# Spreading row gathers over expert blocks, and moving key and value copies to ScalarE, in an attention and mixture-of-experts kernel

## The chip, the cores and the metric

The kernel runs on one core of a Trainium2 chip. A core has five engines with instruction streams of their own: TensorE (PE in the profile; its weight loads are PEld), VectorE (DVE), ScalarE (ACT), GpSimd (POOL) and SyncE (SP), the last of which only issues DMA transfers here. They wait for each other through semaphores. The metric is the time of one execution on the device in microseconds (us); lower is better. All data is float32.

## The reference

Two stages follow each other. The first is attention with a local window and a few global keys, the second a mixture of eight experts in which each token goes to exactly one expert and none is dropped.

```python
# attention: q, k, v are (4, 8, 768, 64); n_global = 8, n_local = 96
scores = q @ k.T / sqrt(64)
rel = pos[:, None] - pos[None, :]
is_global = pos[None, :] < n_global
is_local = (rel >= 0) & (rel < n_local)
keep = is_global | is_local
dist = where(is_global & ~is_local, n_local, abs(rel))
scores = where(keep, scores - slope[h] * dist, -1e9)
out = softmax(scores) @ v
x = out.transpose(0, 2, 1, 3).reshape(3072, 512)

# experts: w_gate (512, 8), w1 (8, 512, 1024), w2 (8, 1024, 512)
logits = x @ w_gate
expert_idx = argmax(logits, axis=1)
gate_w = softmax(logits)[arange(N), expert_idx]
for e in range(8):                       # rows of each expert
    h = maximum(x[expert_idx == e] @ w1[e], 0)
    y[expert_idx == e] = h @ w2[e]
out = gate_w[:, None] * y
```

## The kernel before

Attention goes through 16 pairs of heads (4 batches, 4 pairs each) in three steps per pair, 48 steps in all. A step covers two blocks of 128 queries. Its work is a pipeline over steps: the score products of step n, the attend products (probabilities times values) of step n-2, the transposes of step n-4. As the window is shorter than a block, each block of queries needs its own key block and the one before, whose first 16 columns are replaced by the 16 first keys (the global ones). These replaced copies are `kA` for the keys and `va` for the values; GpSimd makes them:

```python
def keys_at(kT, kA, a0, a1):
    nc.gpsimd.tensor_copy(out=kA[:, a0:a1, GW:P], in_=kT[...][:, :, GW:P])
    nc.gpsimd.tensor_copy(out=kA[:, a0:a1, 0:GW], in_=kT[:, 0:GW]...to_broadcast(...))

def turn_v(pr):
    nc.gpsimd.tensor_copy(out=to, in_=vh[:, :, 0:VA])
    nc.gpsimd.tensor_copy(out=to[0:GW, ...], in_=vh[0:GW, ...].to_broadcast(...))

def scores(n):
    ...                                   # score products into PSUM
    nc.scalar.activation(e, ps, AF.Exp, scale=D ** -0.5)
    if c == 0:
        nc.vector.tensor_tensor(out=e, in0=e, in1=W[...], op=ALU.mult)
    else:
        for h in range(2):                # one mask product per head
            nc.vector.tensor_tensor(out=eh, in0=eh, in1=W[:, 2 * j + h, P:3 * P]..., op=ALU.mult)
```

Attention writes its rows to `x_tok` in device memory. When the last batch is routed, the kernel knows which rows belong to which expert. It fetches them by gathers: an indirect DMA that GpSimd issues, 128 pieces of 512 bytes each, through a list of row numbers. Expert 0 has its first 256 rows computed early (in pieces called by `work(...)`, two blocks at a time), as filler in the tail of attention. The tail and the gathers:

```python
def gather(xq, cols, n, top=N):
    for i in range(n):
        nc.gpsimd.indirect_dma_start(out=xq[:, i, :], in_=x_tok[...], in_offset=...cols[:, i:i + 1]...)

def take(p):                              # all the gathers of expert p, at once
    if p < E:
        xqs[p] = xq_s[p % 2]
        gather(xqs[p], rows_s[...], pieces_of(CAPS[r + 1]))     # 9 to 13 gathers

# ---- tail of attention (nu = 48 steps) ----
turn_x(xe_0, xq_0[0], TB)                 # VectorE turns gathered rows
turn(nu - 3)
attend(nu - 1)
turn_x(xe_0[:, :, P:2 * P], xq_0[1], TB)
work(2)
turn(nu - 2); logits(nu - 3); turn(nu - 1)
work(1)
logits(nu - 2); logits(nu - 1)
work(1)
...                                       # routing, with work pieces between
fetch_0(1)                                # 7 gathers: expert 0's other rows
settle(); work(1); rows_of(...)
take(1)                                   # 13 gathers: expert 1
...
work(3)
turn_x(xe_0, xq_0[0], TB)
work(4)
turn_x(xe_0[:, :, P:2 * P], xq_0[1], pieces_of(C0) - TB)
while later: later.pop(0)()               # two scatters of finished rows
```

Each expert has a hidden product with eight blocks, each followed by a ReLU on ScalarE, and a result product with four blocks, each copied out by VectorE. PSUM holds three blocks of each. The rows of a result are turned back by TensorE, scaled by VectorE and scattered to the output by GpSimd (`turn`), after the first block of the next hidden product. The weights of the next expert come in by SyncE (`fetch`).

```python
def hidden(p, between=None):
    for fc in range(FC):                  # FC = 8
        for kc in range(KC):
            nc.tensor.matmul(ph[:, 0:C], lhsT=w1t[...], rhs=xe[:, kc, 0:C], ...)
        nc.scalar.activation(hT[:, fc, 0:C], ph[:, 0:C], AF.Relu)
        if fc == 0 and between:
            between()                     # turn(): scale and scatter the rows before

def result(p):
    for dc in range(KC):                  # KC = 4
        for fc in range(FC):
            nc.tensor.matmul(po[:, 0:C], lhsT=w2t[...], rhs=hT[:, fc, 0:C], ...)
        nc.vector.tensor_copy(out=yT[:, dc, 0:C], in_=po[:, 0:C])
    return turn

fetch(1, 0); fetch(1, 1); ground()
sort(1)                                   # VectorE turns expert 1's rows
take(2)
hidden(0)
turn = result(0)
for p in range(1, E):
    hidden(p, turn)
    fetch(p + 1, 0)
    sort(p + 1)
    take(p + 2)
    turn = result(p)
    fetch(p + 1, 1)
```

Of the kernel before, what the change touches and what calls it, by code (L numbers as in the profile page):

```python
# [11 lines left out]
AF = mybir.ActivationFunctionType  # L12
# [11 lines left out]
NQ = 4  # L24
# [5 lines left out]
def kernel(  # L30
# [169 lines left out]
    def pieces_of(c):  # L200
        return (c + 31) // 32
# [50 lines left out]
    def rows_of(ps, nm, ns, mw, to_rows):  # L252
# [3 lines left out]
        nc.vector.tensor_scalar(out=to_rows, in0=pw, scalar1=float(NJ), scalar2=j_of[:, 0:1], op0=ALU.mult, op1=ALU.add)  # L256

    def gather(xq, cols, n, top=N):

        for i in range(n):  # L260
            nc.gpsimd.indirect_dma_start(out=xq[:, i, :], out_offset=None, in_=x_tok[0:NJ * top, :],  # L261
                                         in_offset=bass.IndirectOffsetOnAxis(ap=cols[:, i:i + 1], axis=0),
                                         bounds_check=NJ * top - 1, oob_is_err=False)

# [4 lines left out]

    def take(p):  # L270
        if p < E:
            r = ORDER[p] - 1
            xqs[p] = xq_s[p % 2]
            gather(xqs[p], rows_s[:, NQ * TB * r:NQ * TB * r + NQ * TB], pieces_of(CAPS[r + 1]))

# [51 lines left out]
    def banded_attention():  # L327
        with ExitStack() as actx:
# [71 lines left out]
            def turn_v(pr):  # L400
                vt = vts[pr % NV]
                va = vas[pr % 2]
                to = va[:, 0:2 * VA].rearrange("p (h x) -> p h x", h=2)
                vh = vt[:, 0:2 * VT].rearrange("p (h x) -> p h x", h=2)
                nc.gpsimd.tensor_copy(out=to, in_=vh[:, :, 0:VA])  # L405
                nc.gpsimd.tensor_copy(
                    out=to[0:GW, :, VW:VA].rearrange("p h (c w) -> p h c w", w=VW),
                    in_=vh[0:GW, :, 0:VW].rearrange("p h (o w) -> p h o w", o=1).to_broadcast([GW, 2, NB - 2, VW]))
# [43 lines left out]
            def scores(n):  # L452
                b, j, c = units[n]
                qT, kT, kA, _, _ = pairs[b * NJ + j]
# [12 lines left out]
                if n == 0:  # L467
                    turn_first(2, NB, ps_s.tile([P, 2, 512], F32, tag="s", name="first_1"))
                elif c == 1 and b == 0 and j + 1 < NJ:
                    weights(j + 1)  # L470
                if c == 0:
                    nc.vector.tensor_tensor(out=e[:, :, 0:w], in0=e[:, :, 0:w], in1=W[:, 2 * j:2 * j + 2, 0:w],
                                            op=ALU.mult)
                else:
                    for h in range(2):
                        eh = e[:, h, :].rearrange("p (t c) -> p t c", t=2)
                        nc.vector.tensor_tensor(  # L477
                            out=eh, in0=eh,
                            in1=W[:, 2 * j + h, P:3 * P].rearrange("p (o c) -> p o c", o=1).to_broadcast([P, 2, 2 * P]),
                            op=ALU.mult)  # L480
                st[n] = e

            def attend(n):
                b, j, c = units[n]
                _, _, _, vt, va = pairs[b * NJ + j]
                pt = st.pop(n)
# [229 lines left out]
            weights(0)  # L716
            turn_v(0)
            nu = len(units)
# [5 lines left out]
            for n in range(nu + 1):  # L724
# [234 lines left out]
    with tc.manual_schedule():  # L959
# [18 lines left out]
        with ExitStack() as ectx:  # L978
# [29 lines left out]
            def hidden(p, between=None):  # L1008
# [4 lines left out]
                for fc in range(FC):  # L1013
                    ph = ps_h.tile([P, 512], F32, tag="ph", name=f"ph_{p}_{fc}")
                    for kc in range(KC):
                        nc.tensor.matmul(ph[:, 0:C], lhsT=w1t[:, 0, kc, P * fc:P * fc + P], rhs=xe[:, kc, 0:C],  # L1016
                                         start=(kc == 0), stop=(kc == KC - 1))
                    nc.scalar.activation(hT[:, fc, 0:C], ph[:, 0:C], AF.Relu)  # L1018
# [8 lines left out]
            def result(p):  # L1027
# [31 lines left out]
            sort(1)  # L1059
            take(2)  # L1060
            hidden(0)
            turn = result(0)
            pf = ps_t.tile([P, DM], F32, tag="pt", name="pf")
            nc.tensor.matmul(pf[:, 0:1], lhsT=ones, rhs=bad, start=True, stop=True)
            nc.vector.tensor_scalar(out=bad_i, in0=pf[:, 0:1], scalar1=P - 0.5, scalar2=None, op0=ALU.is_lt)
            for p in range(1, E):
                hidden(p, turn)
                fetch(p + 1, 0)
                sort(p + 1)
                take(p + 2)  # L1070
                turn = result(p)
# [71 lines left out]
```

## Time and profile before

| | before |
|---|---|
| time, median of 3 runs | 591.25 us (590.97 to 591.64) |
| span of the profiled execution | 589.4 us |
| mean granted TensorE clock | 0.964 |
| score and attend products begin in earnest | 14.0 us |
| early pieces of expert 0 begin | 182.3 us |
| hidden product of expert 0 (remaining rows), first matmul | 222.4 us |
| its result product, first matmul | 260.2 us |
| result product of expert 7, end of its matmuls | 578.5 us |

The page of a profile has a table of busy times, then the span in 40 equal slices whose digits are tenths of busy time (9 is 90% or more), then groups of instructions by source line. A line such as `L1018 ACT ACTIVATE hT<-ph` names source line, engine, operation, output and input tile. In the view in order of time the first column is the start and the second the duration, both in us; brackets give how long the engine had been idle and what ended that. In the table of windows there are, for each stretch, its length, the busy time of PE, PEld, DVE, ACT and POOL with counts, the granted clock, the share of the DMA engines and GB/s. In the table of waits the numbers are total us, times and longest us; "remote" stands for a releaser that the profile cannot name. Matmul ends are modelled, not recorded.

```profile
q1 hardware_dynamic: 137344, 58.16, 47.4%
q0 software_dynamic: 5264, 12.59, 6.7%
```

These are the DMA queues: packets, MB and share of the 16 engines. The second is GpSimd's, which carries the gathers and scatters.

### The profile page before, as it was taken

Reading aid. Unit: us, or ns where it says so; the run is one execution under the profiler, and the core shown is the slowest. Engines: PE = TensorE matmul, PEld = TensorE weight load, DVE = VectorE, ACT = ScalarE, POOL = GpSimd, SP = SyncE. Lnnn points to the kernel's source line nnn. Section 1 sums busy time; section 2 is a strip of 40 time slices with the busy share of each in tenths; the row PEclk is TensorE's granted clock in tenths of the full one; section 3 lists DMA queues with packets and bytes.
Section 4 is the critical chain, followed back from the end, with each engine's and each line's share of the span. In section 5 each row is a group of like instructions: output and inputs, shape, how many; then the busy total and the mean of one; then the engine's idle time right before and its main releaser. Section 6 shows DMA issues by size and latency. Waiting matters only on the chain.

```text
span 589.4 us, 8006 instructions
## 1 busy us (share of the span) xinstructions
PE 532.9 (90%) x3066; PEld 386.7 (66%) x3066; DVE 205.5 (35%) x537; ACT 101.4 (17%) x197; POOL 176.8 (30%) x227
## 2 busy tenths in 40 slices
PE   3999999999999985089999999999999969999993
PEld 2998988988988834087555555555555747666662
DVE  3886886876862533003003101301301302102011
ACT  2544334333332100010100100110110100100100
POOL 4332214231243077702701720710640640101001
PEclk9999999999999997579999999999999979999998
DMA  9999999999503087129173353562534737201001
GB/s 146 146 143 185 233 186 152 231 144 181 158 12 133 2 172 239 49 54 259 53 149 125 112 114 88 188 123 44 207 82 90 220 75 186 92 1 39 13 1 55
DMA packets 145184, 71.95 MB, mean 122 GB/s; under 512 B 126656, under 2 KB 126660, under 8 KB 145136
## 3 DMA queue, kind: packets, MB, share of 16 engines
q1 hardware_dynamic: 137344, 58.16, 47.4%
q0 software_dynamic: 5264, 12.59, 6.7%
q10 hardware_dynamic: 2528, 0.59, 0.7%
q8 instruction: 26, 0.43, 0.3%
q14 instruction: 22, 0.18, 0.1%
HBM read 59.00 MB, written 12.65 MB: 122 GB/s over the span
## 4 chain that ended last, share of the span: by engine, by line
PE 75%; another core or an unknown queue 11%; DVE 5%; DMA 3%; SPq 2%; issue 1%; ACT 1%; POOL 1%; ACTq 0%; POOLq 0%; DVEq 0%
PE po L1043 26%; PE ph L1016 24%; PE o L495 10%; PE s L463 7%; PE ph L298 3%; PE px L511 2%; PE pt L1052 2%; SPq L362 2%; DMA vt<-in_v_dram 1%; DVE y L287 1%; PE pi L603 1%; PE pq L526 1%; DMA x_tok<-xr 1%; PE pl L539 1%
## 5 line engine op out<-in xcount | busy, mean ns | idle before, releaser
L1045 DVE COPY yT<-po 128x416 f32<-128x416 f32 (+4 forms) x32 | 16.9, 529 | 280.9 <-PE po L1043 280.9
L1016 PE MATMUL ph<-xe,w_first 128*128 128x208 f32 (+3 forms) x256 | 80.8, 477 | 25.5 <-ACT hT L1018 18.7
L261 POOL DMA_INDIRECT xq_s<-x_tok,rows_s x85 | 85.1, 1001 | 25.9 <-issue 24.4
L1043 PE MATMUL po<-hT,w_second 128*128 128x416 f32 (+3 forms) x256 | 81.2, 478 | 5.6 <-ACT hT L1018 5.6
L1016 PEld LDWEIGHTS ph<-xe,w_first 128*128 128x128 f32 x256 | 51.1, 204 | 53.5 <-ACT hT L1018 19.3
L1018 ACT ACTIVATE hT<-ph 128x416 f32<-128x416 f32 (+4 forms) x64 | 29.8, 467 | 324.9 <-PE ph L1016 212.9
L279 POOL DMA_INDIRECT out_dram<-y,idx_s x25 | 24.2, 969 | 204.3 <-DVE y L287 200.9
L1016 PE MATMUL ph<-xe,w_second 128*128 128x416 f32 (+3 forms) x256 | 79.7, 470 | 0.0
L1043 PE MATMUL po<-hT,w_first 128*128 128x208 f32 (+3 forms) x256 | 75.5, 456 | 0.0
L1043 PEld LDWEIGHTS po<-hT,w_second 128*128 128x128 f32 x256 | 49.5, 194 | 36.7 <-issue 10.2
L495 PE MATMUL o<-vt,e 128*128 128x128 f32 x384 | 72.1, 276 | 0.0
L1016 PEld LDWEIGHTS ph<-xe,w_second 128*128 128x128 f32 x256 | 48.3, 190 | 28.6 <-issue 9.8
L1043 PEld LDWEIGHTS po<-hT,w_first 128*128 128x128 f32 x256 | 47.8, 190 | 27.1 <-issue 10.0
L495 PE MATMUL o<-va,e 128*128 128x128 f32 x320 | 62.7, 278 | 0.0
L466 ACT ACTIVATE e<-s 128x1024 f32<-128x1024 f32 (+1 forms) x48 | 45.6, 951 | 94.3 <-issue 47.3
L495 PEld LDWEIGHTS o<-vt,e 128*128 128x128 f32 x384 | 57.0, 192 | 1.5 <-issue 1.0
L477 DVE TENSOR_TENSOR e<-e,Wb 128x512 f32<-128x512 f32 x64 | 45.3, 750 | 15.4 <-ACT e L466 15.2
L495 PEld LDWEIGHTS o<-va,e 128*128 128x128 f32 x320 | 48.5, 192 | 2.6 <-issue 2.5
L463 PE MATMUL s<-qT,kT 64*128 64x128 f32 x384 | 40.7, 290 | 0.9 <-ACT qT L397 0.9
L463 PE MATMUL s<-qT,kA 64*128 64x128 f32 x320 | 35.6, 300 | 3.6 <-POOL kA L381 3.6
L463 PEld LDWEIGHTS s<-qT,kT 64*128 64x128 f32 x384 | 30.8, 196 | 2.8 <-ACT qT L397 1.3
L405 POOL COPY va<-vt 128x650 f32<-128x650 f32 x16 | 14.6, 913 | 57.1 <-DMA vt<-in_v_dram 46.8
(163 smaller groups left out, 433.7 us busy)
## 6 DMA issues: line engine op xcount, KB each, us to landing
w_second<-in_moe_w_dram SPq DMA_DIRECT2D x16, 512.0 KB, 9.5
w_second<-in_moe_w_dram SPq DMA_DIRECT2D x4, 2048.0 KB
x_tok<-xr SPq DMA_DIRECT2D x24, 256.0 KB, 3.5
w_first<-in_moe_w_dram SPq DMA_DIRECT2D x12, 512.0 KB, 7.7
w_first<-in_moe_w_dram SPq DMA_DIRECT2D x3, 2048.0 KB
vt<-in_v_dram SPq DMA_DIRECT2D x31, 192.0 KB, 4.7
qb<-in_q_dram SPq DMA_DIRECT2D x60, 96.0 KB, 4.3
kb<-in_k_dram SPq DMA_DIRECT2D x60, 96.0 KB, 3.7
```

Of the source, the lines that this page charges most:

```text
L261: nc.gpsimd.indirect_dma_start(out=xq[:, i, :], out_offset=None, in_=x_tok[0:NJ * top, :], in_offset=bass.IndirectOffsetOnAxis(ap=cols[:, ...
L279: p = nc.gpsimd.indirect_dma_start(out=out[:, :], out_offset=bass.IndirectOffsetOnAxis(ap=where, axis=0), in_=y[0:rows, :], in_offset=None ...
L298: nc.tensor.matmul(ph[:, P * f:P * f + P], lhsT=w1_0[:, 0, kc, c0:c0 + P], rhs=xe_0[:, kc, P * q:P * q + P], start=(kc == 0), stop=(kc == ...
L405: nc.gpsimd.tensor_copy(out=to, in_=vh[:, :, 0:VA])
L463: nc.tensor.matmul(ps[:, h, P * m:P * m + P], lhsT=lhsT, rhs=qT[r, P * i:P * i + P], start=True, stop=True)
L466: nc.scalar.activation(e[:, :, 0:w], ps[:, :, 0:w], AF.Exp, scale=D ** -0.5)
L477: nc.vector.tensor_tensor(out=eh, in0=eh, in1=W[:, 2 * j + h, P:3 * P].rearrange("p (o c) -> p o c", o=1).to_broadcast([P, 2, 2 * P]), op= ...
L495: nc.tensor.matmul(po[:, t, h, :], lhsT=pt[:, h, P * m:P * m + P], rhs=(vt if own else va)[:, c0:c0 + P], start=(m == mine[0][0]), stop=(m ...
L1016: nc.tensor.matmul(ph[:, 0:C], lhsT=w1t[:, 0, kc, P * fc:P * fc + P], rhs=xe[:, kc, 0:C], start=(kc == 0), stop=(kc == KC - 1))
L1018: nc.scalar.activation(hT[:, fc, 0:C], ph[:, 0:C], AF.Relu)
L1043: nc.tensor.matmul(po[:, 0:C], lhsT=w2t[:, 0, fc, P * dc:P * dc + P], rhs=hT[:, fc, 0:C], start=(fc == 0), stop=(fc == FC - 1))
L1045: nc.vector.tensor_copy(out=yT[:, dc, 0:C], in_=po[:, 0:C])
```

## The change

Three things are changed together.

1. `take(p)` is split. `plan(p)` only puts the gathers of an expert on a list, and `pace(n, after)` issues n of them, each made to wait for a given instruction: one after each ReLU of a hidden product (all that are left after the last), two after the first copy of a result product and one after each other. Expert 1's gathers are still issued at once by `take(1)`. The plan for expert 2 comes after `hidden(0)`. It is meant to keep GpSimd's queue from holding long dense runs of gathers.
2. The key and value copies go from GpSimd to ScalarE, one step later each, and the mask of a step is multiplied by one instruction for both heads. It is meant to keep GpSimd away from VectorE's operands in attention.
3. In the tail the three early pieces of expert 0 that stood around the last turns are put behind them, and the transposes of gathered rows are put together.

```diff
+    pending = []
+
+    def plan(p):
         if p < E:
             r = ORDER[p] - 1
             xqs[p] = xq_s[p % 2]
-            gather(xqs[p], rows_s[:, NQ * TB * r:NQ * TB * r + NQ * TB], pieces_of(CAPS[r + 1]))
+            cols = rows_s[:, NQ * TB * r:NQ * TB * r + NQ * TB]
+            for i in range(pieces_of(CAPS[r + 1])):
+                pending.append((xqs[p], cols, i))
+
+    def pace(n, after):
+        for _ in range(min(n, len(pending))):
+            g = gather_one(*pending.pop(0))
+            tc.add_manual_dep(g.ins, after.ins.name, ...Sync, DATA...)
+
+    def take(p):
+        plan(p)
+        while pending:
+            gather_one(*pending.pop(0))
...
             def keys_at(kT, kA, a0, a1):
-                nc.gpsimd.tensor_copy(out=kA[:, a0:a1, GW:P],
+                nc.scalar.copy(out=kA[:, a0:a1, GW:P],
...
-                nc.gpsimd.tensor_copy(out=kA[:, a0:a1, 0:GW],
+                nc.scalar.copy(out=kA[:, a0:a1, 0:GW],
...                                       # the two value copies likewise
-                keys_at(kT, kA, 0, NB - 1)          # in turn_qk, at c == 0
...
                 if n == 0:
                     turn_first(2, NB, ...)
+                    turn_v(0)
...
-                    for h in range(2):
-                        eh = e[:, h, :].rearrange("p (t c) -> p t c", t=2)
-                        nc.vector.tensor_tensor(out=eh, in0=eh, in1=W[:, 2 * j + h, P:3 * P]..., op=ALU.mult)
+                    eh = e.rearrange("p h (t c) -> p h t c", t=2)
+                    nc.vector.tensor_tensor(out=eh, in0=eh, in1=W[:, 2 * j:2 * j + 2, P:3 * P]..., op=ALU.mult)
...
                 if n < nu and c == 1 and pr + 1 < B * NJ:
+                    keys_at(*pairs[pr + 1][1:3], 0, NB - 1)
+                if n < nu and c == 2 and pr + 1 < B * NJ:
                     turn_v(pr + 1)
...
-            turn_x(xe_0, xq_0[0], TB)
             turn(nu - 3)
             attend(nu - 1)
-            turn_x(xe_0[:, :, P:2 * P], xq_0[1], TB)
-            work(2)
             turn(nu - 2)
             logits(nu - 3)
+            turn_x(xe_0, xq_0[0], TB)
+            turn_x(xe_0[:, :, P:2 * P], xq_0[1], TB)
             turn(nu - 1)
-            work(1)
+            work(3)
             logits(nu - 2)
             logits(nu - 1)
...
             turn_x(xe_0, xq_0[0], TB)
+            turn_x(xe_0[:, :, P:2 * P], xq_0[1], pieces_of(C0) - TB)
             work(4)
-            turn_x(xe_0[:, :, P:2 * P], xq_0[1], pieces_of(C0) - TB)
...
-                    nc.scalar.activation(hT[:, fc, 0:C], ph[:, 0:C], AF.Relu)
+                    done = nc.scalar.activation(hT[:, fc, 0:C], ph[:, 0:C], AF.Relu)
                     if fc == 0 and between:
                         between()
+                    pace(1 if fc < FC - 1 else len(pending), done)
...
-                    nc.vector.tensor_copy(out=yT[:, dc, 0:C], in_=po[:, 0:C])
+                    pace(2 if dc == 0 else 1, nc.vector.tensor_copy(out=yT[:, dc, 0:C], in_=po[:, 0:C]))
...
-            take(2)
             hidden(0)
+            plan(2)
             turn = result(0)
...
                 sort(p + 1)
-                take(p + 2)
+                plan(p + 2)
                 turn = result(p)
```

More of the change, by code (lines that the diff above doesn't have):

```diff
@@ L256, in rows_of, with gather_one @@
         nc.vector.tensor_scalar(out=to_rows, in0=pw, scalar1=float(NJ), scalar2=j_of[:, 0:1], op0=ALU.mult, op1=ALU.add)
+    def gather_one(xq, cols, i, top=N):
+        return nc.gpsimd.indirect_dma_start(out=xq[:, i, :], out_offset=None, in_=x_tok[0:NJ * top, :],
+                                            in_offset=bass.IndirectOffsetOnAxis(ap=cols[:, i:i + 1], axis=0),
+                                            bounds_check=NJ * top - 1, oob_is_err=False)
     def gather(xq, cols, n, top=N):
         for i in range(n):
-            nc.gpsimd.indirect_dma_start(out=xq[:, i, :], out_offset=None, in_=x_tok[0:NJ * top, :],
-                                         in_offset=bass.IndirectOffsetOnAxis(ap=cols[:, i:i + 1], axis=0),
-                                         bounds_check=NJ * top - 1, oob_is_err=False)
+            gather_one(xq, cols, i, top)
     def turn_x(xe, xq, n):
@@ L268, in turn_x @@
             nc.vector.transpose(xe[:, :, 32 * i:32 * i + 32], xq[:, i, :].rearrange("p (k q) -> p k q", k=KC))
-    def take(p):
+    pending = []
+    def plan(p):
         if p < E:
@@ L273, in take @@
             xqs[p] = xq_s[p % 2]
-            gather(xqs[p], rows_s[:, NQ * TB * r:NQ * TB * r + NQ * TB], pieces_of(CAPS[r + 1]))
+            cols = rows_s[:, NQ * TB * r:NQ * TB * r + NQ * TB]
[4 more added lines that the diff above has]
+            g = gather_one(*pending.pop(0))
+            tc.add_manual_dep(g.ins, after.ins.name, mybir.DependencyInfo(mybir.DependencyClass.Sync, mybir.DependencyReason.DATA),
+                              reason="spreads the gathers over the experts' work")
+    def take(p):
+        plan(p)
+        while pending:
+            gather_one(*pending.pop(0))
     scatters = []
@@ L404, in turn_v @@
                 vh = vt[:, 0:2 * VT].rearrange("p (h x) -> p h x", h=2)
-                nc.gpsimd.tensor_copy(out=to, in_=vh[:, :, 0:VA])
-                nc.gpsimd.tensor_copy(
+                nc.scalar.copy(out=to, in_=vh[:, :, 0:VA])
+                nc.scalar.copy(
                     out=to[0:GW, :, VW:VA].rearrange("p h (c w) -> p h c w", w=VW),
@@ L453, in scores @@
                 b, j, c = units[n]
-                qT, kT, kA, _, _ = pairs[b * NJ + j]
+                qT, kT, kA = pairs[b * NJ + j][0:3]
                 bl = blocks(c)
@@ L474, in scores @@
                 else:
-                    for h in range(2):
-                        eh = e[:, h, :].rearrange("p (t c) -> p t c", t=2)
[L477 to L480, printed above, removed]
+                    eh = e.rearrange("p h (t c) -> p h t c", t=2)
+                    nc.vector.tensor_tensor(
+                        out=eh, in0=eh,
+                        in1=W[:, 2 * j:2 * j + 2, P:3 * P].rearrange("p h (o c) -> p h o c", o=1).to_broadcast([P, 2, 2, 2 * P]),
+                        op=ALU.mult)
                 st[n] = e
@@ L484, in attend @@
                 b, j, c = units[n]
-                _, _, _, vt, va = pairs[b * NJ + j]
+                vt, va = pairs[b * NJ + j][3:5]
                 pt = st.pop(n)
@@ L716, in banded_attention @@
             weights(0)
-            turn_v(0)
             nu = len(units)
```

## The prediction

> **What bounds the kernel now.** I read the page's busy table and its 40 slices first. TensorE is busy nearly everywhere, with one hole:
>
> ```profile
> PE 532.9 (90%) x3066; PEld 386.7 (66%) x3066; DVE 205.5 (35%) x537; ACT 101.4 (17%) x197; POOL 176.8 (30%) x227
> ...
> PE   3999999999999985089999999999999969999993
> ...
> POOL 4332214231243077702701720710640640101001
> ```
>
> A slice is 14.7 us. Slices 1 to 12 are attention, 13 to 15 the routing tail with early pieces of expert 0, the rest the eight experts (numbered here by their place in the order, 0 to 7). The hole is slices 15 and 16 (the 8, 5 and 0), and POOL is dense there; a second dip (the 6) is in slice 32, again beside POOL. Second, the table of waits names who held the hole:
>
> ```profile
> ACT hT L1018 <- remote: 70.6, 9, 26.7
> ```
>
> This line is ScalarE's ReLU of the first expert product, waiting for something that the profile cannot name. Third, ScalarE alone in order of time, first around the hole, then around the dip:
>
> ```profile
> 204.14 0.38 ACT L300 ACTIVATE hT<-ph 128x256 f32<-128x256 f32 x1 [2.91 <-PE ph L298]
> 231.23 0.34 ACT L1018 ACTIVATE hT<-ph 128x208 f32<-128x208 f32 x1 [26.71 <-remote]
> 252.14 0.34 ACT L1018 ACTIVATE hT<-ph 128x208 f32<-128x208 f32 x1 [20.56 <-remote]
> ```
>
> ```profile
> 465.66 0.40 ACT L1018 ACTIVATE hT<-ph 128x272 f32<-128x272 f32 x1 [1.44 <-issue]
> 469.13 0.40 ACT L1018 ACTIVATE hT<-ph 128x272 f32<-128x272 f32 x1 [3.07 <-remote]
> 472.71 0.40 ACT L1018 ACTIVATE hT<-ph 128x272 f32<-128x272 f32 x1 [3.18 <-remote]
> 477.69 0.40 ACT L1018 ACTIVATE hT<-ph 128x272 f32<-128x272 f32 x1 [4.58 <-remote]
> 481.94 0.40 ACT L1018 ACTIVATE hT<-ph 128x272 f32<-128x272 f32 x1 [3.86 <-remote]
> ```
>
> The second ReLU waits for TensorE alone in the program. In the order of time TensorE began block 0 at 222.36, and blocks 0 to 2 stand as done by 228.5; yet their ReLUs run at 231.23, 252.14 and 254.29. With three PSUM buffers TensorE can do block 3 and then stops until 252.53. Fourth, the dense stretch in the table of windows:
>
> ```profile
> 235.00:250.00 15.00, 0.00 (x0) 0.00 (x0) 0.00 (x0) 0.00 (x0) 11.65 (x12) 0.50 0.19 52
> ```
>
> Every compute engine is idle and only POOL works, at gathers. The POOL rows of that stretch are 13 gathers from 233.45 to 250.11; the stuck ReLU goes 2.0 us after the last one ends. Around the dip 12 gathers run from 464.17 to 479.53, and the last stuck ReLU goes at 481.94, 2.4 us later. Experts 2 to 4 show the same on a small scale: expert 4's last gather ends at 434.9, its last ReLU comes at 437.25, some 3 us late, without cost, as TensorE has other work. Expert 1's 13 gathers (278.73 to 295.4) delayed nothing. So: **signals from TensorE reach ScalarE late while a dense run of gathers is on, and are through about 2.4 us after the run.** Why the hardware does so no row tells; I take it as a regularity of this trace. The signals to VectorE are late too beside the first 8 gathers (171.7 to 182.6): the normalisations at 180.78 and 183.81 follow products whose rows ended about 2 us and 3 us earlier.
>
> **What the Trainium skill says.** "Perfetto Trace Analysis", section "DMA Instruction — SWDGE (GPSIMD)": the end of a GpSimd DMA in a profile is that of descriptor generation, not of the transfer. The trace agrees: a gather's row is 1.00 us, and its consumers go later. The same page, "Tensor Engine Instruction (MATMUL, LD_WEIGHTS)": a matmul's end is computed, and its semaphore is pushed only once PSUM has acknowledged. So a finished row at 228.5 doesn't prove that the signal had left; this fits the trace, which proves neither. "SBUF — State Buffer", "Who interferes with whom": a VectorE instruction with two SBUF inputs contends with a GpSimd instruction that reads SBUF. It agrees: the pair of mask products at 33.44 took 2.30 us beside POOL's value and key copies, and takes 1.29 us undisturbed. No page I found bears on late TensorE signals.
>
> **The change, part by part.**
>
> *Gathers of expert 2, out of the first hidden product.* Before, all 13 stand on POOL right after the first scatters and so beside hidden(0). After, they follow hidden(0), paced by result(0) and hidden(1). But 7+13 gathers for experts 0 and 1 stay in one run: before, 204.76 to 230.5, then two scatters to 233.1. So the first ReLU still comes at about 231. What follows is freed once the remaining run is through: at best 230.5 + 2.4 = 233, if the scatters count like gathers 233.1 + 2.4 = 235.5. From the second ReLU to the last took 260.42 - 252.14 = 8.3 us before, cold clock included. hidden(0) then ends between 233 + 8.3 = 241 and 235.5 + 8.3 = 244, against 260.4: 16 to 19 us saved, middle 17.5.
>
> *Gathers of the later experts, one per block.* In hidden(5) the blocks are 1.83 us. Before: 4 scatters and 12 gathers in a row. After: 4 scatters, then 7 gathers (5 have moved into result(4)): 11 x 1.3 us from 459.1 ends near 473.4, so the late signals are through by 476. TensorE's result product of expert 5 began at 472.80, and its 64 matmuls need 64 x 0.229 = 14.7 us (1.83 us for the 8 of a block), so it would end near 487.5 and ended at 495.5: 8 us lost, of which I count 7.5 saved. In hidden(2) to hidden(4) TensorE lost nothing, so nothing is won. The last gather of 13 now starts after the last ReLU of its block; its 1 us, about 2.4 us of landing and the transposes end some 4 us into the result product, whose first copy is due at 5.6 us and has three PSUM buffers. No loss.
>
> *Copies from POOL to ScalarE.* ScalarE copies of 256 and 512 columns last 0.367 and 0.580 us, so 0.154 + 0.000832 per column. Key copies (560 and 80 columns) and value copies (650 and 520): 0.62 + 0.22 + 0.70 + 0.59 = 2.13 us per pair of heads, 16 pairs. ScalarE has 2 x 1.02 + 0.81 + 3 x 0.37 = 3.96 us per pair in a period of 9.07 us: it goes to 6.1, and fits. At the start the second key copy no longer stands behind the first value copy: TensorE waited for it from 10.4 to 13.99, and after qT (11.74) plus 0.8 us of copies it can go at 12.5: 1.5 us saved. That is mostly taken back: ScalarE now waits in order for the third value load (on POOL it landed at 32.55), and the exp that ran at 28.98 then runs at about 33.9. TensorE needs it by 34.3, so the lead is gone and perhaps 0.4 us with it.
>
> *One mask product instead of two.* From 0.650 us for 512 and 0.948 for 768 columns, 1024 cost 1.25 against 1.29: nothing. Without POOL beside it VectorE regains about 45.3 - 32 x 1.25 = 5 us, but TensorE sets the pace (49.28 of 50 us busy between 100 and 150). I count 0.7 us at each of three batch boundaries, 2 us. Attention in all: -1.5 us, between -5 and +2.
>
> *Tail.* Three early expert pieces move behind the last turns and the transposes. Before, two of them (182.28 to 186.1) filled the wait for the last normalisation at 184.45; now TensorE idles there about 2.5 us, and the logits come after three pieces: 184.9 + 3 x 1.85 + 1.1 + one piece = 193.5 for the sums that began at 191.8. +1.5 us, passed on to the gather run by routing.
>
> Sum: 591.25 - 17.5 - 7.5 - 1.5 + 1.5 = 566; with a small loss for imperfect pacing **567 us**.
>
> **Rivals.** (1) *The late signals survive*: the run for experts 0 and 1 is still 20 gathers and two scatters, and what heals it may be something else, such as the second expert's weights, whose 4 MB load the engines to 233. If only the second ReLU's gap halves, 10 us are saved there: about 575. Against it: at the dip the DMA share is 0.18, and the signals were late just the same. (2) *ScalarE becomes the brake of attention*: it waits in order for value loads, which POOL waited 46.8 us for. In later pairs the landing coincides with the next exp (47.06 against 47.12, 57.05 against 57.31), so a delay is about 1.3 us and under the two-step lead. Were it not hidden, 16 x 0.5 = 8 us: 575. (3) *All late signals vanish*: hidden(0) would start at 222.4 + 1 and take 8 x 1.4 = 11.3 us: 235. That gives 558. (4) *VectorE blocks on the last gather* ahead of the result copies; landing would have to exceed 12 us. I count it small.
>
> **Range and chances.** The single terms spread by some 4 us (hidden(0)), 2.5 (expert 5), 3 (attention), 1.5 (tail): together 6. With the rivals to both sides: 557 to 579. 2% faster is 579.4; 0.88 for that, 0.10 for within, 0.02 for slower.
>
> **What would show it.** Right: no POOL rows besides hidden(0)'s second half, the gap between the first two ReLUs of hidden(0) under 4 us instead of 20.6, hidden(0) over about 16 us earlier, expert 5's ReLUs 1.8 us apart or nearly, its result product without pauses, the period of a pair still about 9.1 us. Wrong: "remote" waits of over 10 us that remain, or an attention that ends later than before by more than 3 us with ScalarE idle on value loads.

## The result, and the profile after

The changed kernel takes **568.79 us** (median of 4 runs, 565.80 to 569.01) against **591.44 us** for the kernel before on the same chip (4 runs, 590.97 to 593.37): ratio **0.9602**, 95% interval 0.9568 to 0.9636. The prediction was 567 us.

The page of the changed kernel, busy table and slices (a slice is 14.1 us):

```profile
PE 530.0 (94%) x3066; PEld 385.3 (68%) x3066; DVE 203.4 (36%) x505; ACT 132.7 (24%) x263; POOL 137.4 (24%) x161
...
PE   4989999999999997599999999999999999999993
...
POOL 5000000000006047324324422523502544402002
```

TensorE does the same 3066 matmuls in nearly the same busy time (530.0 against 532.9 us); what went is idle time. The hole is now a 7 and a 5, where it was 8, 5 and 0; the dip late in the experts is gone; and behind the run ahead of hidden(0) POOL's 6s and 7s have become 2s to 5s. ScalarE has taken over 31 us of copies. In the table of waits the line that the prediction rested on (70.6 us in 9 waits) has become:

```profile
ACT hT L1036 <- remote: 10.6, 1, 10.6
```

ScalarE in order of time, around hidden(0), the hidden product of expert 0 (start, duration, instruction, idle time before it and who ended it):

```profile
203.56 0.38 ACT L319 ACTIVATE hT<-ph 128x256 f32<-128x256 f32 x1 [2.91 <-PE ph L317]
224.36 0.34 ACT L1036 ACTIVATE hT<-ph 128x208 f32<-128x208 f32 x1 [20.42 <-issue]
235.26 0.82 ACT L1036 ACTIVATE hT<-ph 128x208 f32<-128x208 f32 x3 [10.55 <-remote]
238.78 0.34 ACT L1036 ACTIVATE hT<-ph 128x208 f32<-128x208 f32 x1 [2.71 <-PE ph L1034]
240.19 0.34 ACT L1036 ACTIVATE hT<-ph 128x208 f32<-128x208 f32 x1 [1.06 <-PE ph L1034]
```

and POOL's last rows before 235.26, and the next one after them:

```profile
228.96 0.99 POOL L260 DMA_INDIRECT xq_s<-x_tok,rows_s  x1 [0.30 <-issue]
230.26 1.02 POOL L298 DMA_INDIRECT out_dram<-y,idx  x1 [0.30 <-issue]
231.58 1.01 POOL L298 DMA_INDIRECT out_dram<-y,idx  x1 [0.31 <-issue]
246.46 1.05 POOL L260 DMA_INDIRECT xq_s<-x_tok,rows_s  x1 [13.88 <-DVE yT L1064]
```

The dense run is shorter by expert 2's 13 gathers. Its last member, a scatter, ends at 232.59, and 2.7 us later three stuck ReLUs go at once. From then on the ReLUs follow TensorE. The rest of the run (7 gathers for expert 0, 13 for expert 1, two scatters) still costs a hole of 6.8 us.

From rows of this kind the whole difference between the two profiles can be laid out by stage. The last exp is the start of ScalarE's last exponential of attention scores, and result(5) is the result product of expert 5:

| stage | before, us | after, us | difference | predicted |
|---|---|---|---|---|
| to the last exp of attention | 175.39 | 175.67 | +0.3 | -1.5 |
| tail, to hidden(0)'s first matmul | 46.97 | 45.62 | -1.35 | +1.5 |
| hidden(0), to result(0)'s first matmul | 37.86 | 21.51 | -16.35 | -17.5 |
| result(0) to the start of result(5) | 212.58 | 212.58 | 0.0 | 0 |
| result(5) | 22.71 | 14.83 | -7.9 | -7.5 |
| everything after | 93.9 | 93.9 | 0.0 | 0 |

The sum is -25.3, which is the difference of the spans (589.4 and 564.1). The profiled execution of the changed kernel was the fastest of its four (565.80 us); a second profile below, from another set of runs, shows a wait of 2.2 us that this one does not have.

### The profile page after: what moved, and what is told of

Its sections match the earlier page's. It is cut to its first block, busy times and chain, and to the rows that moved or that the text cites. A ratio compares the mean times of both kernels' runs of the same rounds, so it can differ in the third digit from the quotient of the medians.

```text
span 564.1 us, 7989 instructions
## 1 busy us (share of the span) xinstructions
PE 530.0 (94%) x3066; PEld 385.3 (68%) x3066; DVE 203.4 (36%) x505; ACT 132.7 (24%) x263; POOL 137.4 (24%) x161
## 4 chain that ended last, share of the span: by engine, by line
PE 74%; DMA 7%; DVE 7%; SPq 5%; another core or an unknown queue 2%; ACT 2%; issue 1%; ACTq 1%; POOL 0%; POOLq 0%; DVEq 0%
PE po L1062 27%; PE ph L1034 26%; PE o L513 7%; PE s L481 4%; SPq L381 4%; PE ph L317 3%; DMA w_second<-in_moe_w_dram 2%; PE pt L1071 2%; DMA kb<-in_k_dram 2%; DMA vt<-in_v_dram 2%; PE px L529 2%; DVE y L306 1%; PE pi L621 1%; DVE qT L434 1%
## 5 line engine op out<-in xcount | busy, mean ns | idle before, releaser
L1034 PE MATMUL ph<-xe,w_first 128*128 128x208 f32 (+3 forms) x256 | 79.5, 471 | 10.0 <-ACT hT L1036 6.8
L1062 PE MATMUL po<-hT,w_second 128*128 128x416 f32 (+3 forms) x256 | 78.9, 469 | 0.0
L1062 PEld LDWEIGHTS po<-hT,w_second 128*128 128x128 f32 x256 | 48.6, 190 | 29.7 <-issue 10.2
L1062 PEld LDWEIGHTS po<-hT,w_first 128*128 128x128 f32 x256 | 47.7, 190 | 27.1 <-issue 10.2
L271 DVE STREAM_TRANSPOSE xe<-xq_s 128x128 f32<-128x128 f32 x85 | 23.6, 296 | 116.3 <-DMA xq_s<-x_tok,rows_s 114.4
L260 POOL DMA_INDIRECT xq<-x_tok,rows x15 | 16.9, 1124 | 188.3 <-DVE early L645 164.1
L495 DVE TENSOR_TENSOR e<-e,Wb 128x1024 f32<-128x1024 f32 x32 | 38.7, 1212 | 17.3 <-ACT e L484 17.2
```

Of the source, the lines that this page charges most:

```text
L260: return nc.gpsimd.indirect_dma_start(out=xq[:, i, :], out_offset=None, in_=x_tok[0:NJ * top, :], in_offset=bass.IndirectOffsetOnAxis(ap=c ...
L271: nc.vector.transpose(xe[:, :, 32 * i:32 * i + 32], xq[:, i, :].rearrange("p (k q) -> p k q", k=KC))
L495: nc.vector.tensor_tensor(out=eh, in0=eh, in1=W[:, 2 * j:2 * j + 2, P:3 * P].rearrange("p h (o c) -> p h o c", o=1).to_broadcast([P, 2, 2, ...
```

## The experiments

Each set of runs below sits on one chip together with the kernel before, so its ratio is safe; but the sets fell on different chips, five in all, and that turned out to matter more than any edit. On three of them (second, fourth and fifth set) the kernel before takes 592 to 595 us, as in the comparison above (591.44), whose chip is not on record. On the other two (first and third set) it takes 558.5 us. I call the first kind chips with late signals and the other chips in time; each chip was met once, so whether it is a property of the chip or of the hour there, the runs do not tell.

**First set: the parts one by one.** e1_pacing is the kernel before with `plan` and `pace` alone; e2_copies with key and value copies on ScalarE and the single mask product; e3_tail with the new tail order alone. e4_dense_after holds expert 2's gathers to the end of hidden(0), but then runs them densely:

```diff
+                    done = nc.scalar.activation(hT[:, fc, 0:C], ph[:, 0:C], AF.Relu)
+                    if fc == FC - 1:
+                        pace(len(pending), done)
...
-            take(2)
+            plan(2)
             hidden(0)
```

> The kernel before with the pacing alone (plan and pace; copies, mask product and tail order as before). Theory (the dense run of gathers holds TensorE's signals back): nearly the whole gain is here, hidden(0) ends near 244 us instead of 260.4, expert 5 no longer loses its 8 us, time 567 to 570 us. Rival A (what helps is that POOL is rid of the key and value copies): no more than 5 us, 586 us or above. Rival B (the new order of the tail gives it): the same, 586 us or above.

> The kernel before with the key and value copies on ScalarE and the single mask product, no pacing, old tail. Theory: attention 0 to 2 us earlier, the hole of 20 us in hidden(0) stays: 589 to 592 us. Rival (ScalarE becomes the brake of attention): 594 us or more, and the last exp of attention over 3 us later than 175.4. Rival A of the first run: 570 us.

> The kernel before with the new order of the tail alone. The prediction counted +1.5 us for it, so 593 us; in the trace of the changed kernel hidden(0) began 1.1 us earlier than before although attention's last exp came 0.3 us later, which says about -1.3 us, so 590 us. The second is what I now expect. The hole in hidden(0) stays either way.

> The kernel before, and only expert 2's 13 gathers are held back until hidden(0)'s last ReLU; then they run in one dense row beside result(0). Later experts as before. If freeing hidden(0) is the whole of the first term: hidden(0) ends near 244 us, expert 5 still loses 8 us, and the time is 575 us (591.4 - 16.5). If a dense run is harmful wherever it stands: VectorE's copies of result(0) come late up to 2.4 us after the run, near 264 instead of 257, and the time is 579 to 582 us. If the stuck signals come from something else than these gathers (the load of the second expert's weights up to 233 us): hidden(0) still ends near 260, 591 us.

Measured, against 558.52 us for the kernel before (47 runs): e1_pacing 558.99 (ratio 1.0004, 0.9987 to 1.0021), e2_copies 558.08 (1.0010, 0.9990 to 1.0030), e3_tail 558.57 (0.9994, 0.9976 to 1.0013), e4_dense_after 558.43 (0.9995, 0.9982 to 1.0009). No theory had this: no part is worth anything, and the kernel before is itself 33 us faster. The profile of e2_copies, where all gathers stand as before, shows why. ScalarE, then POOL:

```profile
223.04 0.34 ACT L1018 ACTIVATE hT<-ph 128x208 f32<-128x208 f32 x1 [19.27 <-PE ph L1016]
224.32 0.34 ACT L1018 ACTIVATE hT<-ph 128x208 f32<-128x208 f32 x1 [0.94 <-PE ph L1016]
225.73 0.34 ACT L1018 ACTIVATE hT<-ph 128x208 f32<-128x208 f32 x1 [1.06 <-PE ph L1016]
```

```profile
222.31 1.00 POOL L261 DMA_INDIRECT xq_s<-x_tok,rows_s  x1 [0.30 <-issue]
223.61 1.00 POOL L261 DMA_INDIRECT xq_s<-x_tok,rows_s  x1 [0.30 <-issue]
224.92 1.00 POOL L261 DMA_INDIRECT xq_s<-x_tok,rows_s  x1 [0.30 <-issue]
```

The same dense run with the same rows of 1.00 us and the same 1.30 us from start to start lies beside all of hidden(0), and not one signal is late: hidden(0) takes 11.33 us. (In the other profiles on chips in time it takes 12.74 to 14.37 us, with TensorE's clock granted at 0.50 for part of it, as in e1_pacing from 222 to 224 us; here it is granted in full.) So a dense run is not enough for the hole. What e4_dense_after was to tell, whether a dense run beside result(0) does harm, stays open: it ran only where nothing is late.

What this set does tell is what the other parts cost when nothing is stuck. From the last exp to hidden(0)'s first matmul the old tail takes 44.96, 45.11 and 44.89 us (e1_pacing, e2_copies, e4_dense_after), the new one 45.64 (e3_tail): the new order costs 0.6 us there.

**Second set: is it the chip, and is it the run?** r5_after is the changed kernel itself. w1_split thins the run that is left ahead of hidden(0): six of expert 1's gathers stay, seven follow hidden(0)'s ReLUs, and the two scatters stand behind them:

```diff
-            take(1)
+            plan(1)
+            for _ in range(6):
+                gather_one(*pending.pop(0))
...
-            sort(1)
             hidden(0)
+            while later:
+                later.pop(0)()
+            sort(1)
             plan(2)
```

w2_weights is the changed kernel in which the first DMA of expert 1's weights waits for VectorE's check of the normalisations, which stands behind the first expert's transposes:

```diff
-            fetch(1, 0)
+            fetch(1, 0, ground())
             fetch(1, 1)
-            ground()
```

> The changed kernel, unedited, timed against the kernel before once more, because in the four runs so far the kernel before took 558.5 us and its hole did not exist. If the hole belongs to the chip or the hour and not to the program: where the kernel before takes about 558.5 us the change is worth nothing (ratio 0.998 to 1.002), and where it takes about 591 us the ratio is 0.96 again. If the four edits only failed because each was alone: ratio 0.96 to 0.98 even where the kernel before takes 558.5 us.

> The changed kernel, and 7 of expert 1's 13 gathers and the two early scatters are also taken out of the run ahead of hidden(0): the 7 follow its ReLUs one by one. Theory where signals come late: the run ends at 221 us, hidden(0) ends near 235 instead of 243 us, time 560 to 562 us against 568.8. Where signals are in time: nothing, within 1 us of the changed kernel.

> The changed kernel, and expert 1's 4 MB of weights wait until the first expert's rows are transposed, 221 us instead of 209. In the traces hidden(0) starts some 3.2 us after TensorE is free, held by gathers that land while the weights load. Expected: the last of them lands near 216 us, hidden(0) starts at about 218.3 instead of 221.3, and 3 us are won: 555.5 us where the kernel before takes 558.5. If gathers land late for another reason than the weights: 558.5, nothing. If late signals, where they exist, come from the weights' load: hidden(0) ends there at about 235.

Measured, against 594.57 us for the kernel before (7 runs): r5_after **570.10** (0.9581, 0.9548 to 0.9615), w1_split **560.00** (0.9427, 0.9372 to 0.9481), w2_weights 570.78 (0.9593, 0.9557 to 0.9628). On this chip signals are late, and the change is worth again what it was. w1_split's ReLUs in hidden(0):

```profile
224.00 0.34 ACT L1037 ACTIVATE hT<-ph 128x208 f32<-128x208 f32 x1 [19.40 <-PE ph L1035]
225.28 0.34 ACT L1037 ACTIVATE hT<-ph 128x208 f32<-128x208 f32 x1 [0.94 <-PE ph L1035]
...
230.90 0.34 ACT L1037 ACTIVATE hT<-ph 128x208 f32<-128x208 f32 x1 [1.06 <-PE ph L1035]
233.33 0.73 ACT L1037 ACTIVATE hT<-ph 128x208 f32<-128x208 f32 x2 [2.09 <-PE ph L1035]
```

The run pauses at 221.5, and hidden(0) takes 11.33 us, as in e2_copies on a chip in time: the run was what cost the changed kernel its remaining 10 us. (In result(0) 1.2 us are lost again, by the wait that is shown at the end of this set.) In w2_weights hidden(0) does start as soon as TensorE is free: from the last exp it takes 42.31 us instead of 45.53. But it is then stuck until the run ends:

```profile
224.26 0.34 ACT L1040 ACTIVATE hT<-ph 128x208 f32<-128x208 f32 x1 [16.78 <-PE ph L1038]
238.98 0.81 ACT L1040 ACTIVATE hT<-ph 128x208 f32<-128x208 f32 x3 [14.38 <-remote]
```

The last scatter ends at 236.18 there, 2.8 us earlier. The early start is given back in full, and the rival that blamed the load of the weights falls: their issue was moved from 209.02 us to 222.83 us, and the signals still go 2.8 us after the run's end, while the weights load on at full rate (DMA share 1.02 from 238 to 242 us).

This set also shows a new wait that the change makes. VectorE in r5_after around result(5):

```profile
463.95 0.31 DVE L271 STREAM_TRANSPOSE xe<-xq_s 128x128 f32<-128x128 f32 x1 [6.59 <-DMA xq_s<-x_tok,rows_s]
470.17 0.31 DVE L271 STREAM_TRANSPOSE xe<-xq_s 128x128 f32<-128x128 f32 x1 [5.91 <-DMA xq_s<-x_tok,rows_s]
470.41 1.10 DVE L1064 COPY yT<-po 128x272 f32<-128x272 f32 x3
```

and TensorE, SyncE and POOL's last paced gather beside it:

```profile
457.81 11.16 PE L1062 MATMUL po<-hT,w_second 128*128 128x272 f32 x48
470.86 3.94 PE L1062 MATMUL po<-hT,w_second 128*128 128x272 f32 x16 [1.89 <-DVE yT L1064]
```

```profile
458.00 1.96 SPq L241 DMA_DIRECT2D w_second<-in_moe_w_dram  x4
```

```profile
458.98 1.00 POOL L260 DMA_INDIRECT xq_s<-x_tok,rows_s  x1 [0.30 <-issue]
```

This gather was released by a ReLU that was itself late, and it now starts behind the first of the next expert's weights, which SyncE begins to issue at 458.00, when hidden(5) is done. It lands some 10 us after its row; in the first profile of the changed kernel the last gather's row ended at 456.83, the weights' issue began at 456.60, and VectorE had the rows at 459.77. VectorE, in order, waits for it ahead of the result's copies; three product blocks fill the three PSUM buffers, and TensorE stops for 1.89 us. result(5) lasts 16.99 us instead of 14.83. It is 17.10 in w1_split and 17.32 in w2_weights.

**Third set: density, on a chip in time.** e1_pacing_b is e1_pacing again. g_gap is the kernel before, nothing paced, with a short clearing of a scratch tile ahead of each gather:

```diff
-            gather(xqs[p], rows_s[:, NQ * TB * r:NQ * TB * r + NQ * TB], pieces_of(CAPS[r + 1]))
+            cols = rows_s[:, NQ * TB * r:NQ * TB * r + NQ * TB]
+            for i in range(pieces_of(CAPS[r + 1])):
+                nc.gpsimd.memset(gap, 0.0)
+                gather(xqs[p][:, i:i + 1, :], cols[:, i:i + 1], 1)
```

> The kernel before with the pacing alone, once more, because the first try fell on a chip where the kernel before takes 558.5 us and no signal is late. Where the kernel before takes 591 us or more: the pacing carries the gain, 569 to 572 us (ratio 0.962 to 0.967), and copies, mask product and tail together are worth no more than 2 us, the rest up to the changed kernel's 0.958. Rival (copies or tail carry part of it): ratio above 0.97. Where the kernel before takes 558.5 us: nothing again.

> The kernel before, nothing paced, but ahead of each gather of experts 1 to 7 POOL clears 512 columns of a scratch tile, about 0.5 us, so that the gathers start 1.8 us apart instead of 1.3. Where signals come late: if it is the density of the run that holds them (a hole between gathers lets them through), the ReLUs of hidden(0) come 1.4 us apart, hidden(0) ends by 240 us although gathers stand beside all of it, and the time is 560 to 570 us. If it is that gathers are queued at all, or that POOL is busy, the run is only longer, ends near 262 instead of 250 us, and hidden(0) with it: 600 us or more. Where no signal is late: within 1 us of the kernel before.

Measured, against 558.58 us (39 runs): e1_pacing_b 558.67 (1.0003, 0.9987 to 1.0019), g_gap 559.03 (1.0014, 0.9995 to 1.0032). A chip in time again, and inconclusive, but for the remark that 85 clearings of 0.54 us cost nothing there.

**Fourth set: the parts, where it counts.** e1_pacing_c is e1_pacing once more; w3_both is w1_split and w2_weights together.

> The kernel before with the pacing alone, a third try for a chip where signals come late. There: 569 to 572 us or a ratio of 0.962 to 0.967, with the rest up to 0.958 for copies, mask product and tail. Rival (copies or tail carry part of the gain): ratio above 0.97. Where the kernel before takes 558.5 us: nothing, as twice before.

> The changed kernel with both later edits: 7 of expert 1's gathers and the early scatters out of the run ahead of hidden(0), and expert 1's weights held until the first expert's rows are transposed. Where signals are in time: hidden(0) starts 3 us earlier, 555.5 to 557 us against 558.5. Where they are late: the 3 us at the start may be lost again, as the 7 gathers now land while the weights load and VectorE waits for the last of them ahead of result(0)'s copies; 558 to 561 us, no better than w1_split's 560.0.

Measured, against 594.73 us (7 runs): e1_pacing_c **571.36** (0.9620, 0.9581 to 0.9660), w3_both **557.58** (0.9367, 0.9335 to 0.9398). The pacing alone carries the gain. ScalarE in e1_pacing_c's hidden(0):

```profile
234.80 0.34 ACT L1037 ACTIVATE hT<-ph 128x208 f32<-128x208 f32 x1 [28.18 <-remote]
238.25 0.82 ACT L1037 ACTIVATE hT<-ph 128x208 f32<-128x208 f32 x3 [3.11 <-remote]
```

The run ends at 235.32 here, and hidden(0) takes 20.43 us. Copies, mask product and tail together are the difference between 0.962 and r5_after's 0.958, some 2 us on another chip and within the two intervals. e1_pacing_c has the old tail, and there the stretch from last exp to hidden(0) is 46.89 us, as in the kernel before (46.97), while the changed kernel has 45.62 and 45.53: where signals are late, its tail is 1.4 us shorter. Whether the new order or the moved copies do that is not separated (see the part on the tail below).

w3_both is the fastest kernel of the study where signals are late, and a little faster than expected (558 to 561 us): the early start is not lost again. It is 42.31 us from the last exp to hidden(0), hidden(0) takes 12.39 us, and the kernel pays 3.8 us in result(5), which lasts 18.65 us, for the wait shown above.

**Fifth set: density, where it counts.** g_gap_b is g_gap, unedited.

> The kernel before with half a microsecond of clearing a scratch tile ahead of each gather of experts 1 to 7 (1.7 us from gather to gather instead of 1.3), a second try for a chip where signals come late. There: if the density of the run holds the signals, hidden(0) ends by 240 us with gathers beside all of it, and the time is 560 to 570 us; if it is the run as such, or a busy POOL, the run only grows, to about 258, and hidden(0) with it: 600 us or more. Where signals are in time: within 1 us of the kernel before, as in the first try.

Measured, against 592.27 us (7 runs): **562.35 us** (0.9497, 0.9445 to 0.9550). POOL, then ScalarE, in hidden(0):

```profile
228.99 0.54 POOL L277 MEMSET gap<- 128x512 f32 x1
229.69 1.01 POOL L262 DMA_INDIRECT xq_s<-x_tok,rows_s  x1 [0.16 <-issue]
230.69 0.55 POOL L277 MEMSET gap<- 128x512 f32 x1
231.40 1.01 POOL L262 DMA_INDIRECT xq_s<-x_tok,rows_s  x1 [0.17 <-issue]
```

```profile
226.94 0.34 ACT L1022 ACTIVATE hT<-ph 128x208 f32<-128x208 f32 x1 [20.73 <-PE ph L1020]
229.58 0.34 ACT L1022 ACTIVATE hT<-ph 128x208 f32<-128x208 f32 x1 [2.30 <-PE ph L1020]
231.13 0.34 ACT L1022 ACTIVATE hT<-ph 128x208 f32<-128x208 f32 x1 [1.20 <-PE ph L1020]
232.54 0.34 ACT L1022 ACTIVATE hT<-ph 128x208 f32<-128x208 f32 x1 [1.06 <-issue]
```

Gathers stand beside every block of hidden(0), and POOL is busier than it ever was (12.4 of the 14 us from 224 to 238). Yet no ReLU waits for more than its block. The 2.30 ahead of the second goes with TensorE's clock, granted at 0.52 on average from 224 to 230 and in full afterwards; on the chip in time g_gap's hidden(0) takes the same 14.3 us. Expert 5's ReLUs are 1.83 us apart from the second on, and result(5) lasts 14.83 us; the gathers that VectorE needs there end at 417.54, long before, and those for expert 7 stand beside it without harm. So neither a busy POOL nor gathers beside the products are enough to hold the signals. In hidden(0) and around result(5) gathers that follow each other every 1.30 us hold them, and gathers that come every 1.71 us, with a clearing between, do not. Whether the time between the gathers or the clearing itself does it was not separated.

## Why the prediction was right, and where it was not

**The regularity** ("signals from TensorE reach ScalarE late while a dense run of gathers is on, and are through about 2.4 us after the run") held in hidden(0) wherever a dense run stood beside it on a chip with late signals: 2.7 us after the run in the changed kernel, 3.0 in r5_after, 2.8 in w2_weights, 2.9 in e1_pacing_c and 2.1 in w3_both. The scatters count like gathers, which the prediction had left open. It was taken for a property of the program and is not one: on two chips of five the same run delayed nothing. The prediction had no chance of seeing that, as it had one trace. But rival (3), *all late signals vanish*, "gives 558", and 558.5 is what the kernel before itself takes where they do. That the changed kernel was timed on the chip of the trace is luck for the number: on a chip in time the parts of the change are worth nothing.

**First term**, hidden(0) ends "between 241 and 244": it ended at 242.80, and the stage got 16.35 us shorter against 17.5. Two details failed. The first ReLU was to come "still at about 231" and came at 224.36, without effect, as the second was stuck until 235.26. And two signs that were to show the step right failed. A gap of under 4 us between the first two ReLUs followed from the first one at 231, and became 10.9 us as that one came early. No remote wait of over 10 us could not be expected by the prediction's own reckoning: it left 20 gathers in the run, and its own first ReLU at 231 would have come 27 us after the one before. The remote wait was 10.6 us (28.18 us in e1_pacing_c, where the first ReLU did come late).

**Second term**, expert 5: -7.9 us against -7.5. result(5) ran without a pause in the first profile, and of the five intervals between these ReLUs of expert 5 four are under 1.9 us and one is 3.57:

```profile
446.42 0.40 ACT L1036 ACTIVATE hT<-ph 128x272 f32<-128x272 f32 x1 [1.44 <-PE ph L1034]
448.25 0.40 ACT L1036 ACTIVATE hT<-ph 128x272 f32<-128x272 f32 x1 [1.44 <-issue]
450.13 0.40 ACT L1036 ACTIVATE hT<-ph 128x272 f32<-128x272 f32 x1 [1.49 <-PE ph L1034]
453.70 0.40 ACT L1036 ACTIVATE hT<-ph 128x272 f32<-128x272 f32 x1 [3.17 <-PE ph L1034]
455.17 0.40 ACT L1036 ACTIVATE hT<-ph 128x272 f32<-128x272 f32 x1 [1.07 <-PE ph L1034]
456.61 0.40 ACT L1036 ACTIVATE hT<-ph 128x272 f32<-128x272 f32 x1 [1.03 <-PE ph L1034]
```

The step "about 2.4 us of landing ... No loss" is the one that failed: r5_after shows 10 us of landing behind the weights and 2.2 us lost. Rival (4), *VectorE blocks on the last gather*, was said to need a landing of over 12 us; 10 were enough, because the gather's row itself, released late, ended only 2.2 us into result(5). This is of the size by which the other executions of the changed kernel lie above the profiled one (568.7 to 569.0 against 565.8); that it is the same wait in each of them was not seen.

**Attention**, -1.5 us: +0.3. The start did what was said: the second exp came at 14.66 instead of 15.96, and the seventh at 32.28 instead of 28.98 (33.9 was predicted). The term that was mis-sized is "0.7 us at each of three batch boundaries": from the 13th exp (47.12, after 47.74) to the 25th (90.86, after 91.16) 0.3 us came back, from there to the 37th (134.21, after 134.53) nothing. Rival (2), ScalarE as brake, did not come: e2_copies is at 1.0010.

The single mask product was priced right (1.25 us; the page has it in the group below), and ScalarE's copies too: 0.743, 0.629, 0.662 and 0.262 us make 2.30 us per pair against 2.13.

```profile
L495 DVE TENSOR_TENSOR e<-e,Wb 128x1024 f32<-128x1024 f32 x32 | 38.7, 1212 | 17.3 <-ACT e L484 17.2
...
L424 ACT COPY va<-vt 128x650 f32<-128x650 f32 x16 | 11.9, 743 | 7.4 <-DMA vt<-in_v_dram 7.4
L425 ACT COPY va<-vt 16x520 f32<-16x520 f32 x16 | 10.1, 629 | 0.5
L398 ACT COPY kA<-kT 128x560 f32<-128x560 f32 x15 | 9.9, 662 | 1.7 <-DVE kT L433 1.7
```

**Tail**, +1.5 us: -1.35. The failed step is that TensorE "idles there about 2.5 us" until a last normalisation at 184.45. That time was itself a late signal: counted from the last exp, the last two normalisations come at 5.40 and 8.42 us in the kernel before, but at 3.66 and 5.66 in e1_pacing, which has the same tail on a chip in time. In the changed kernel they come at 3.70 and 5.71. The new order need not be what freed them, because its first 8 gathers are also less dense. Two of their rows are longer:

```profile
173.55 2.04 POOL L260 DMA_INDIRECT xq<-x_tok,rows  x1 [0.30 <-issue]
177.19 1.63 POOL L260 DMA_INDIRECT xq<-x_tok,rows  x1 [0.30 <-issue]
```

In the kernel before they last 1.52 and 1.00 us. e2_copies, with the old order, has the longer rows too (2.03 and 1.63), and e3_tail, with the new order alone, does not (1.52 and 1.00). So they come with the copies and the single mask product. Neither of the two edits was run alone on a chip with late signals, and which of them freed the tail stays open. Where nothing is late, the new order costs 0.6 us.

So 567 against 568.8 is partly luck of the sum: attention was counted 1.8 us too well, the tail 2.9 us too badly, hidden(0) 1.2 us too well. The mechanism and the two large terms carried it, 24 of the 25 us.

The mechanism rested on no page of the Trainium skill, and what it did cite held: "Perfetto Trace Analysis", section "DMA Instruction — SWDGE (GPSIMD)", warns that a GpSimd DMA's row ends with the descriptors and not with the transfer, and in r5_after the two are 10 us apart.

## What to carry to other kernels

A wait that the profile puts down to nobody, next to a dense row of gathers on GpSimd, is worth a cheap test before anything is rescheduled: half a microsecond of other work ahead of each gather won 5.0% here, where the change won 4.0 and 4.2%, without touching the order, though each on its own chip. When gathers are paced by another engine's work, the last one must still land before the next bulk load is issued, or whoever waits for it in order can take the loss (2.2 us in r5_after). And a gain that removes waits of unknown origin should be measured on several chips: the pacing is worth 3.8% where signals are late and nothing on two chips of five. (The changed kernel as a whole was not run on a chip in time; each of its parts was.)

## What the runs showed of the hardware that was not expected

- The same program takes 558.5 us on two chips and 592 to 595 us on three, with equal gather rows (1.00 us, 1.30 us apart) and equal product stages: from result(0) to result(5) it is 212.58 us in the profiles of both kinds. The span of the kernel before (589.4) exceeds e2_copies' (553.9, the experts' gathers as before) by 35.5 us, and 26.5 of them lie in hidden(0), 7.9 in result(5) and 1.9 in the tail, where ReLUs, copies and normalisations waited for TensorE's signals, with -0.7 in attention. (In hidden(0) the difference is 23.5 to 26.5 us, depending on the profile in time that is taken.) What makes a chip or its hour so is open.
- One trait goes with the late signals in every profile: the trace lacks records. Of the semaphore steps by which DMA transfers report their landing, the profiles in time hold 5983 to 5990 and the late ones 4308 to 5359, fewest in the kernel before. So the recording of a profile may itself take part in the delay. Every execution here comes with a recorded span and clock, so none shows how the kernels fare without recording.
- Beside dense gathers the signal of a finished product was held for at least 23.6 us (in the kernel before blocks 0 to 2 of hidden(0) stand as done at 228.50, and block 1's ReLU went at 252.14), and it was let go 2.0 to 3.0 us after the last gather or scatter of the run. At 1.71 us from start to start, with a clearing between, nothing was held. Between 1.30 and 1.71 nothing was tried; in w1_split gathers 1.30 to 1.41 us apart, each bound to a ReLU, delayed only the seventh ReLU, by about 1 us. A gather that waits for a ReLU cannot run ahead of a late signal, so those are not the same case as a free run.
- The pace of the products may matter too, which was not tested: the 13 dense gathers beside hidden(1), whose blocks come every 2.79 us, delayed nothing in the kernel before.
- The landing of the last gather ahead of result(5) went from 2.9 us after its row in the first profile of the changed kernel to 10.2 us in r5_after, where the first of 2 MB of weights had been issued 1 us ahead of it. The traces in time record the landings: 1.5 us for several of e1_pacing's paced gathers (rows that end from 441.26 to 446.48), 9.5 us for one of e3_tail's (row that ends at 450.0).

No kernel with gaps ahead of all gathers, the early ones of the tail and expert 0's seven included, together with w2_weights' later load, was run. g_gap_b still shows late normalisations beside the first 8 gathers, and its stretch from last exp to hidden(0) is 45.81 us, against 44.77 for the same program on a chip in time; whether w2_weights' 3 us would come on top is not shown.
